# Mixture-of-experts tail of a fused kernel: a second row buffer for the second layer's output, another dealing of the weight splits, and more GpSimd drains

## The chip, the core and the metric

The kernel runs on one core of one Trainium2 chip. The metric is the device time of one execution in microseconds (us), median of several runs. All times below are in us unless ns is written. The engines are called as in the profile: PE is the matrix engine, PEld its weight loads, DVE the vector engine, ACT the scalar engine, POOL the GpSimd engine, SP the engine that issues most DMAs.

## What is computed

Attention with a compressive memory, then two mixture-of-experts layers in a row. Each layer sends every one of 2304 tokens (512 wide) to one of 8 experts and applies that expert's two matrices:

```python
def _moe2_ref(x, w_gate, w1, w2):              # the first layer differs in its router
    logits = x @ w_gate
    expert_idx = np.argmax(logits, axis=1)
    probs = softmax(logits)
    gate_w = probs[np.arange(N), expert_idx]
    for e in range(E):                          # E = 8, D = 512, F = 1024
        mask = expert_idx == e
        h = np.maximum(x[mask] @ w1[e], 0.0)
        out[mask] = gate_w[mask, None] * (h @ w2[e])
    return out

x = attention(...)            # 2304 x 512
x = _moe_ref(x, ...)          # first layer
return _moe2_ref(x, ...)      # second layer
```

## The kernel before, in words

Each layer (`L` = 0 for the first, 1 for the second) is a row of steps `t` = 0, 1, 2, ...; a step takes 128 rows of one expert. The rows of an expert are gathered by index, so the number of steps depends on the data; in the profiled execution there are 22 in each layer, t = 0 to 21. From t = 18 on, a step stands inside a conditional block, since it may not be needed.

A step (`step`, L1508) multiplies its rows by W1 in two halves (PE accumulates in `ph0` and `ph1`), transposes the result (`hT_pe`), and multiplies it by W2 (accumulated in `py`). To keep float32 accuracy every product is made from a high and a low part: `h` and `l` in the code. So each expert's W1 and W2, once they have come by DMA into `stg` in four chunks each, are *split*: ACT writes the high part of a chunk to `Wh` (`split_hi`, L942) and DVE the low part to `Wl` (`split_lo`, L945). There are two sets of `Wh` and `Wl`, so that the next expert's are written while the present one's are read. Splits stand in conditional blocks (`splits`, L1365, the condition at L1370): only the steps before a change of expert do them. A split chunk costs both engines time, and each engine works through its instructions strictly in the order of the program.

W1's four splits are made one step late, in three places of the next step. I number the places: the **first** at the step's start (L1521, ahead of the evacuation of `ph0` into `hs[0]` at L1530), the **second** after the next step's rows were transposed (L1542), the **third** after `hT_ev(1, ...)` (L1563). Before the change chunks 0 and 1 are done in the first place, chunk 2 in the second, chunk 3 in the third. This holds in both layers, for t from 3 to 17 in the first and for t from 3 on in the second (`shifted`). W2's four splits come later in the same step, all at once (L1588 and following). In the first layer the router of the second layer runs between the third place and W2's splits: `route2` (L1424), a chain of small DVE operations (`mn` L1429, `t8s` L1430) with one ACT operation (`th`, L1435), which starts from the step before's output rows.

At a step's end `end(L, t)` (L1458) scales `py` by the gate into the row buffer `ysb` (ACT, L1460) and POOL sends it out. A step with at most 64 rows is a *half step*: two quarter-work halves are computed, ACT copies one (L1468), DVE adds and scales (L1470, L1471). In the second layer POOL scatters `ysb` to the output by an indirect DMA (L1476) and then, at the start of the next step, gathers the rows for the step after that: four transfers into `xg` (L1211) and one into `xca` (L1212), which holds gate and index. All of POOL's DMAs stand in this one order. The next write of `ysb` waits until the scatter from it has landed. Because the two ways of writing `ysb` stand in conditional blocks of ACT and DVE, the scatter waits until both engines have passed them (L1465, L1469), and each gets there only after all that stands ahead of it in its own order.

In the last step that is sure to run (L = 1, t = 16, the 17th) POOL executes a drain ahead of `end` (L1608 to L1610).

`xg0` is a row buffer of the same size as `ysb`; it takes the gathered rows of step 0 of a layer, and nothing uses it after the second layer's step 0 has transposed them.

Of the kernel before, what the change touches and what calls it, by code (L numbers as in the profile page):

```python
# [11 lines left out]
I32 = mybir.dt.int32  # L12
AF = mybir.ActivationFunctionType
ALU = mybir.AluOpType
# [375 lines left out]
def tile_kernel(ctx, tc, q, k, v, M_prev, z_prev, beta, emb, tau, w1a, w2a, wg, w1b, w2b, out):  # L390
    nc = tc.nc
# [3 lines left out]
    P = 128  # L395
    KD, KF = DM // P, FF // P
    NT1 = NTOK // P
# [11 lines left out]
    x1, x2, a1, a2 = x1a[1:], x2a[1:], a1a[1:], a2a[1:]  # L409

    def ctile(shape, name, dt=F32):
        return cst.tile(shape, dt, name=name)
# [9 lines left out]
    xg0 = ctile([P, DM], "xg0")  # L422
# [803 lines left out]
    psx, pm1, ph1, pt0, pt1, py, pm0, ph0 = (psp.tile([P, 512], F32, name=x) for x in ("psx", "pm1", "ph1", "pt0", "pt1", "py", "pm0", "ph0"))  # L1226
# [42 lines left out]
    HT = P // 2  # L1269
# [187 lines left out]

    def end(L, t):  # L1458
        xc = xca[t % 3 if t else 3]
        whole = lambda: nc.scalar.activation(out=ysb, in_=py, func=AF.Copy, scale=xc[:, 0:1])  # L1460
        hv = steps[L, t].hv
        if hv is None:
            whole()
        else:
            with tc.If(hv[1] < 1) as cmp:  # L1465
                whole()
            with cmp.Else():
                nc.scalar.activation(out=ysb[0:HT], in_=py[HT:P], func=AF.Copy)  # L1468
            with tc.If(hv[0] > 0):  # L1469
                nc.vector.tensor_tensor(out=ysb[0:HT], in0=py[0:HT], in1=ysb[0:HT], op=ALU.add)  # L1470
                nc.vector.tensor_scalar(out=ysb[0:HT], in0=ysb[0:HT], scalar1=xc[0:HT, 0:1], scalar2=None, op0=ALU.mult)  # L1471
        if L == 0:
            nc.gpsimd.tensor_copy(xcb, xc)
            nc.gpsimd.dma_start(out=x2[P * t:P * t + P], in_=ysb)
        else:
            nc.gpsimd.indirect_dma_start(out=out, out_offset=bass.IndirectOffsetOnAxis(ap=xc[:, 1:2].bitcast(I32), axis=0), in_=ysb, in_offset=None,  # L1476
                                         bounds_check=NTOK - 1, oob_is_err=False)

    def hT_pe(i, b):
# [28 lines left out]
    def step(L, t):  # L1508
# [9 lines left out]
        before = steps[L, t - 1]  # L1518
        shifted = 2 < t <= (NT1 - 1 if L == 0 else NS - 1)
        if shifted:  # L1520
            before.splits(0, (0, 1), later=True)  # L1521
        if s.hv is None:
            s.gemm(0, ph0, lx, 0, 0, 3)
            yield
# [14 lines left out]
            yT_pe()  # L1539
            yT_ev(b.hs[0])  # L1540
        if shifted:
            before.splits(0, (2,), later=True)  # L1542
        yield
        rk = L == 0 and 2 <= t <= NT1 - 2
        if rk:
# [14 lines left out]
        s.either(lambda: (s.gemm(1, py, lh, 0, 0, n2), hT_pe(1, b)), lambda: (s.gemm2(1, py, lh, 0, HQ[1][0:4]), hT2_pe(1, b)))  # L1560
        hT_ev(1, b, s.hv)
        if shifted:
            before.splits(0, (3,), later=True)  # L1563
            before.loads(0, range(4))
        if more:
            next_flags(L, t + 1)
# [38 lines left out]
        if more:  # L1605
            steps[L, t + 1].pe_flags()
        last_mm[1] = s.lm
        if (L, t) == (1, NT1 - 2):  # L1608

            nc.gpsimd.drain()  # L1610
        if rt2:
            nc.gpsimd.dma_start(out=a2[P * (t - 1):P * t], in_=xcb)
        end(L, t)
        if rk and ((t - 1) % 6 == 0 or t == NT1 - 2):
            c0 = (t - 2) // 6 * 6
# [122 lines left out]
    ysb = fp.tile([P, DM], F32, name="ysb")  # L1738
# [31 lines left out]
    run(C, 1)  # L1770
    g2b(3)
    end(0, 0)
    next_step(0, 1)
    last_mm[0] = last_mm[1] = s.lm
# [7 lines left out]
    for t in range(1, NS):  # L1782
        if t == NT1 - 1:
            nt_ = rg["nt"] = nc.values_load(ini[0:1, 0, 3:4], min_val=NT1, max_val=NS)
        if t >= NT1:
            nest.enter_context(tc.If(nt_ > t, label=f"tile0_{t}"))
        goes_on(0, t)
        if t == 1:
            abreast(step(0, t), C, (6, 0, 11, 2, 0, 0, 4, 20))
        elif t == 2:  # L1790
            abreast(step(0, t), flags_words(fls[0]), (1,))
        elif t == NT1 - 1:
            rg["wv"] = nc.values_load(ini[0:1, 1, 4:5], engines=[ACT_, DVE_], min_val=0, max_val=1)
            steps[1, 0] = Step(1, 0)
            abreast(step(0, t), choose2(), (5, 3, 0, 1, 2, 1, 1, 1, 1, 1, 1, 1, 0))
        else:
            drain(step(0, t))
# [61 lines left out]
    for i, q_ in enumerate(range(3, 24, 3)):  # L1859
        run(C, n1[4 + i])  # L1860
        if i == 3:
            next_rows(1)
        s.gemm(1, py, lh, 0, q_, q_ + 3)
    end(1, 0)
    next_step(1, 1)
    nest = ExitStack()
# [44 lines left out]
```

## Time and profile before

| what | value |
|---|---|
| median of 3 runs | 864.61 us (863.68 to 866.53) |
| the profiled execution, whole | 866.82 us |
| its span, first to last instruction | 865.1 us |
| PE busy share of the span | 96% |
| DVE, ACT, POOL busy share | 64%, 55%, 52% |
| mean granted clock of PE | 0.995 |

In the profile a row of a timeline gives the start in us from the span's start, the busy time, the engine, the line of the kernel, the operation, what it writes and reads, and how many instructions are merged (x4: four); in square brackets stands how long the engine sat idle before it, and what ended that idle time. An engine's name with a q (ACTq, DVEq) means its sequencer: a branch or a wait that it passed. The first layer's steps run from about 298 to 587 us of the span, the second's from about 603 to the end.

### The profile page before, as it was taken

Reading aid. Unit: us, or ns where it says so; the run is one execution under the profiler, and the core shown is the slowest. Engines: PE = TensorE matmul, PEld = TensorE weight load, DVE = VectorE, ACT = ScalarE, POOL = GpSimd, SP = SyncE. Lnnn points to the kernel's source line nnn. Section 1 sums busy time; section 2 is a strip of 40 time slices with the busy share of each in tenths; the row PEclk is TensorE's granted clock in tenths of the full one; section 3 lists DMA queues with packets and bytes.
Section 4 is the critical chain, followed back from the end, with each engine's and each line's share of the span. In section 5 each row is a group of like instructions: output and inputs, shape, how many; then the busy total and the mean of one; then the engine's idle time right before and its main releaser. Section 6 shows DMA issues by size and latency. Waiting matters only on the chain. (4 is left out here: it accounts for less than half of the span.)

```text
span 865.1 us, 21374 instructions
## 1 busy us (share of the span) xinstructions
PE 827.9 (96%) x5091; PEld 634.3 (73%) x5091; DVE 557.9 (64%) x1671; ACT 478.3 (55%) x940; POOL 448.9 (52%) x526
## 2 busy tenths in 40 slices
PE   5999999999999999999999999998999999999995
PEld 2777777777778778777777777776778878677774
DVE  5666667568686987597747776754676625656721
ACT  3666766766757636475636543632385535656632
POOL 5466755644643346464544545355554456544553
PEclk9999999999999999999999999999999999999998
DMA  8423545622406265385715315211667713667111
GB/s 135 85 42 70 105 79 155 131 42 44 104 5 217 86 223 164 118 273 193 246 45 152 127 42 169 102 53 40 243 200 273 231 51 113 207 192 232 46 40 41
DMA packets 145001, 110.58 MB, mean 128 GB/s; under 512 B 112430, under 2 KB 112430, under 8 KB 144824
## 3 DMA queue, kind: packets, MB, share of 16 engines
q1 hardware_dynamic: 130680, 85.03, 35.1%
q0 software_dynamic: 11776, 23.23, 8.6%
q8 instruction: 70, 1.15, 0.6%
q14 instruction: 107, 0.88, 0.4%
q10 hardware_dynamic: 2368, 0.30, 0.2%
HBM read 90.32 MB, written 19.25 MB: 127 GB/s over the span
## 5 line engine op out<-in xcount | busy, mean ns | idle before, releaser
L1356 PE MATMUL py<-Wh,b 128*128 (+1 forms) x640 | 217.0, 403 | 2.4 <-DVE b L1254 2.4
L1356 PE MATMUL ph<-Wh,b 128*128 (+1 forms) x624 | 210.4, 399 | 2.6 <-issue 1.1
L1211 POOL DMA_INDIRECT xg<-x_scratch,pos x168 | 174.5, 1039 | 69.0 <-issue 48.6
L945 DVE TENSOR_TENSOR Wl<-stg,Wh 128x1024 f32 (+1 forms) x120 | 145.5, 1220 | 43.7 <-ACT Wh L942 35.5
L1356 PEld LDWEIGHTS py<-Wh,b 128*128 128x128 f32 x640 | 119.9, 188 | 35.8 <-issue 7.5
L1356 PEld LDWEIGHTS ph<-Wh,b 128*128 128x128 f32 x624 | 115.9, 188 | 32.5 <-issue 5.8
L1356 PE MATMUL py<-Wl,b 128*128 (+2 forms) x344 | 130.1, 397 | 0.0
L1356 PE MATMUL ph<-Wl,b 128*128 (+2 forms) x336 | 129.6, 392 | 0.0
L942 ACT ACTIVATE Wh<-stg 128x1024 f32 (+1 forms) x120 | 125.6, 1057 | 5.7 <-DMA stg<-in_moe_w_dram 2.3
L1254 DVE SCALAR_TENSOR_TENSOR b<-pt,b 128x512 fp32r<-128x512 f32 (+1 forms) x86 | 56.1, 653 | 93.7 <-ACTq L1370 52.2
L267 ACT ACTIVATE att<-psat 128x512 f32<-128x512 f32 (+1 forms) x144 | 66.7, 463 | 75.9 <-PE psat L265 75.4
L288 PE MATMUL psav<-vb,att 128*128 128x128 f32 (+1 forms) x640 | 93.9, 281 | 0.2 <-ACT att L267 0.2
L288 PEld LDWEIGHTS psav<-vb,att 128*128 128x128 f32 x640 | 80.4, 191 | 17.0 <-ACT att L267 5.2
L1249 ACT ACTIVATE b<-pt 128x512 fp32r<-128x512 f32 x86 | 51.4, 598 | 60.1 <-PE pt L1481 46.6
L248 ACT ACTIVATE a<-a,mx 128x128 f32<-128x128 f32 (+3 forms) x128 | 71.0, 555 | 6.0 <-DVE mx L213 5.7
L213 DVE CUSTOM_DVE_ANT_0 a<-pss,wmask 128x128 f32<-128x128 f32 (+3 forms) x128 | 60.9, 481 | 14.9 <-PE pss L235 13.4
L300 POOL TENSOR_TENSOR xb<-tmp,memx 128x512 f32<-128x512 f32 x15 | 19.1, 1271 | 98.8 <-DVE tmp L299 67.6
L1356 PEld LDWEIGHTS py<-Wl,b 128*128 128x128 f32 (+1 forms) x344 | 61.5, 181 | 11.4 <-ACTq L1370 1.3
L1356 PEld LDWEIGHTS ph<-Wl,b 128*128 128x128 f32 (+1 forms) x336 | 60.6, 180 | 12.4
L1460 ACT ACTIVATE ysb<-py,xca 128x512 f32<-128x512 f32 x38 | 25.9, 682 | 71.4 <-PE py L1356 54.9
L1476 POOL DMA_INDIRECT out_dram<-ysb,xca x22 | 23.9, 1088 | 77.1 <-issue 29.0
L1212 POOL DMA_INDIRECT xca<-a_scratch,idx x48 | 47.5, 989 | 19.1 <-issue 12.8
(404 smaller groups left out, 1330.3 us busy)
## 6 DMA issues: line engine op xcount, KB each, us to landing
stg<-in_moe_w_dram SPq DMA_DIRECT2D x120, 512.0 KB, 9.8
x_scratch<-ysb POOLq DMA_DIRECT2D x22, 256.0 KB
qkn<-in_q_dram SPq DMA_DIRECT2D x64, 72.0 KB, 2.5
qkn<-in_k_dram SPq DMA_DIRECT2D x60, 72.0 KB, 2.3
vb<-in_v_dram SPq DMA_DIRECT2D x32, 128.0 KB, 2.5
x_scratch<-xb SPq DMA_DIRECT2D x16, 256.0 KB, 2.6
x_scratch<-stg SPq DMA_DIRECT2D x11, 256.0 KB, 4.5
xg<-x_scratch,pos POOLq DMA_INDIRECT x168
```

The costliest lines, as they stand in the source:

```text
L213: nc.vector.tensor_tensor_reduce(out=out, in0=ps, in1=mask, scale=-0.125, scalar=bound, op0=ALU.add, op1=ALU.min, accum_out=m)
L248: nc.scalar.activation(out=a[:, 0:N], in_=a[:, 0:N], func=AF.Exp, scale=-1.0, bias=mx, accum_out=rs_t[pi][:, c, j:j + 1])
L267: nc.scalar.activation(out=att[:, 0:N], in_=ps[:, 0:N], func=AF.Copy)
L288: nc.tensor.matmul(av_t[pi][:, c, j:], att[:, 128 * kb:128 * kb + 128], vn[:, kb, j:, 0:D], start=(kb == 0), stop=(kb == c))
L942: return nc.scalar.activation(out=chunk(Wh, c, wv), in_=stg[:, c].unsqueeze(1), func=AF.Copy).ins
L945: return nc.vector.tensor_tensor(out=chunk(Wl, c, wv), in0=stg[:, c].unsqueeze(1), in1=chunk(Wh, c, wv).bitcast(F32), op=ALU.subtract).ins
L1211: ind(out=xgt[t % 2][:, P * k:P * k + P], out_offset=None, in_=quarter, in_offset=bass.IndirectOffsetOnAxis(ap=ix[:, k:k + 1], axis=0))
L1212: ind(out=xca[t % 3 if t else 3], out_offset=None, in_=aux[L][0:n], in_offset=bass.IndirectOffsetOnAxis(ap=idx[:, L, t:t + 1], axis=0))
L1249: nc.scalar.activation(out=hl[:, :, 0:P], in_=ps, func=AF.Relu if relu else AF.Copy)
L1254: nc.vector.scalar_tensor_tensor(out=o, in0=x, scalar=0.0, in1=h, op0=ALU.max, op1=ALU.subtract)
L1356: mm = nc.tensor.matmul(o, x, W, start=(first and q_ == qs[0]), stop=(last and q_ == qs[-1]))
L1460: whole = lambda: nc.scalar.activation(out=ysb, in_=py, func=AF.Copy, scale=xc[:, 0:1])
```

## The change

Three edits, all in `step` and `end`:

1. In the second layer odd steps write their output rows to `xg0`, even ones to `ysb`.
2. W1's splits are dealt 1, 1, 2 to the three places, where they were dealt 2, 1, 1: chunk 1 moves from the first place to the second, chunk 2 from the second to the third. Both layers.
3. POOL's drain ahead of `end`, which was in step 16 of the second layer alone, is in every step of that layer from 16 on.

```diff
     def end(L, t):
         xc = xca[t % 3 if t else 3]
-        whole = lambda: nc.scalar.activation(out=ysb, in_=py, func=AF.Copy, scale=xc[:, 0:1])
+        y = xg0 if L == 1 and t % 2 else ysb
+        whole = lambda: nc.scalar.activation(out=y, in_=py, func=AF.Copy, scale=xc[:, 0:1])
...
-                nc.scalar.activation(out=ysb[0:HT], in_=py[HT:P], func=AF.Copy)
+                nc.scalar.activation(out=y[0:HT], in_=py[HT:P], func=AF.Copy)
...
-            nc.gpsimd.indirect_dma_start(out=out, ..., in_=ysb, in_offset=None,
+            nc.gpsimd.indirect_dma_start(out=out, ..., in_=y, in_offset=None,
...
     def step(L, t):
...
         if shifted:
-            before.splits(0, (0, 1), later=True)
+            before.splits(0, (0,), later=True)
...
         if shifted:
-            before.splits(0, (2,), later=True)
+            before.splits(0, (1,), later=True)
...
         if shifted:
-            before.splits(0, (3,), later=True)
+            before.splits(0, (2, 3), later=True)
             before.loads(0, range(4))
...
-        if (L, t) == (1, NT1 - 2):
+        if L == 1 and t >= NT1 - 2:
             nc.gpsimd.drain()
```

## Rows read from the trace of the kernel before

**Rows 1.** The page's first part: busy us, share of the span, instructions
```profile
PE 827.9 (96%) x5091; PEld 634.3 (73%) x5091; DVE 557.9 (64%) x1671; ACT 478.3 (55%) x940; POOL 448.9 (52%) x526
```

**Rows 2.** Waits of PE, first layer (297 to 587): total us, times, longest
```profile
PE pt L1481 <- ACT hs L1530: 2.8, 2, 1.8
```

**Rows 3.** Waits of PE, second layer (605 to 866)
```profile
PE pt L1481 <- ACT hs L1530: 2.8, 3, 1.6
```

**Rows 4.** Timeline of DVE, first layer, step 7, from the third place on
```profile
388.38 0.68 DVE L1254 SCALAR_TENSOR_TENSOR b<-pt,b 128x512 fp32r<-128x512 f32 x1
388.98 1.21 DVE L945 TENSOR_TENSOR Wl<-stg,Wh 128x1024 f32 x1
390.11 0.16 DVE L1429 TENSOR_REDUCE mn<-pm 128x1 f32<-128x8 f32 x1
```

**Rows 5.** Timeline of ACT, first layer, step 7 from its third place into step 8
```profile
387.46 1.05 ACT L942 ACTIVATE Wh<-stg 128x1024 f32 x1
390.57 0.27 ACT L1435 ACTIVATE th<-pm,mn 128x8 f32<-128x8 f32 x1 [2.06 <-DVE t8s L1430]
390.74 4.34 ACT L942 ACTIVATE Wh<-stg 128x1024 f32 x4
394.99 0.67 ACT L1460 ACTIVATE ysb<-py,xca 128x512 f32<-128x512 f32 x1
395.84 0.60 ACT L1530 ACTIVATE hs<-ph 128x512 f32<-128x512 f32 x1 [0.18 <-ACTq L1370]
```

**Rows 6.** Timeline of PE, first layer: starts of steps 4, 7 and 8
```profile
343.84 0.60 PE L1481 MATMUL pt<-ident,hs 128*128 128x128 f32 x4
...
382.62 0.44 PE L1481 MATMUL pt<-ident,hs 128*128 128x128 f32 x2 [1.83 <-ACT hs L1530]
...
392.22 0.39 PE L1356 MATMUL ph<-Wh,b 128*128 x1
...
396.50 0.66 PE L1481 MATMUL pt<-ident,hs 128*128 128x128 f32 x4
```

**Rows 7.** Timeline of ACT, first layer: the same `hs` of steps 4 and 16
```profile
342.93 0.60 ACT L1530 ACTIVATE hs<-ph 128x512 f32<-128x512 f32 x1 [0.18 <-ACTq L1370]
...
502.97 0.60 ACT L1530 ACTIVATE hs<-ph 128x512 f32<-128x512 f32 x1 [0.18 <-ACTq L1370]
```

**Rows 8.** Timeline of ACT, second layer: ends of steps 11 and 17
```profile
737.61 0.67 ACT L1460 ACTIVATE ysb<-py,xca 128x512 f32<-128x512 f32 x1
738.47 0.60 ACT L1530 ACTIVATE hs<-ph 128x512 f32<-128x512 f32 x1 [0.19 <-ACTq L1370]
...
810.30 0.67 ACT L1460 ACTIVATE ysb<-py,xca 128x512 f32<-128x512 f32 x1
811.45 0.60 ACT L1530 ACTIVATE hs<-ph 128x512 f32<-128x512 f32 x1 [0.47 <-PE ph L1356]
```

**Rows 9.** Timeline of ACT, second layer: ends of steps 12 and 16
```profile
747.96 0.60 ACT L1468 ACTIVATE ysb<-py 64x512 f32<-64x512 f32 x1 [3.73 <-DMA out_dram<-ysb,xca]
...
797.09 0.60 ACT L1468 ACTIVATE ysb<-py 64x512 f32<-64x512 f32 x1 [3.65 <-DMA out_dram<-ysb,xca]
```

**Rows 10.** Timeline of PE, second layer: step 13's stall, then step 17's
```profile
751.77 0.44 PE L1481 MATMUL pt<-ident,hs 128*128 128x128 f32 x2 [1.57 <-ACT hs L1530]
...
800.69 0.66 PE L1481 MATMUL pt<-ident,hs 128*128 128x128 f32 x4 [0.72 <-ACT hs L1530]
```

**Rows 11.** Timeline of POOL, second layer: around the drain, and the last two steps
```profile
797.24 0.95 POOL L1212 DMA_INDIRECT xca<-a_scratch,idx  x1 [0.85 <-DMA out_dram<-ysb,xca]
803.84 1.94 POOL L1476 DMA_INDIRECT out_dram<-ysb,xca  x1 [5.66 <-DVE xTs L1244]
...
845.10 1.02 POOL L1476 DMA_INDIRECT out_dram<-ysb,xca  x1 [4.90 <-ACTq L1370]
...
851.49 0.96 POOL L1212 DMA_INDIRECT xca<-a_scratch,idx  x1 [0.30 <-issue]
857.45 1.02 POOL L1476 DMA_INDIRECT out_dram<-ysb,xca  x1 [5.01 <-ACTq L1879]
```

**Rows 12.** Instructions of L1610, the drain: ns min/median/max, first and last start
```profile
L1610 POOLq DRAIN  x1: 4852/4852/4852, 798.0 to 798.0; - x1
```

**Rows 13.** Instructions of L1905, where the kernel ends: POOL's drains
```profile
L1905 POOLq DRAIN  x3: 46/109/2578, 861.7 to 864.8; - x3
```

**Rows 14.** Timeline of DVE beside the drain of step 16
```profile
799.54 2.54 DVE L945 TENSOR_TENSOR Wl<-stg,Wh 128x1024 f32 x2 [0.63 <-ACT Wh L942]
```

More of the change, by code (lines that the diff above doesn't have):

```diff
@@ L1467, in end @@
             with cmp.Else():
-                nc.scalar.activation(out=ysb[0:HT], in_=py[HT:P], func=AF.Copy)
+                nc.scalar.activation(out=y[0:HT], in_=py[HT:P], func=AF.Copy)
             with tc.If(hv[0] > 0):
-                nc.vector.tensor_tensor(out=ysb[0:HT], in0=py[0:HT], in1=ysb[0:HT], op=ALU.add)
-                nc.vector.tensor_scalar(out=ysb[0:HT], in0=ysb[0:HT], scalar1=xc[0:HT, 0:1], scalar2=None, op0=ALU.mult)
+                nc.vector.tensor_tensor(out=y[0:HT], in0=py[0:HT], in1=y[0:HT], op=ALU.add)
+                nc.vector.tensor_scalar(out=y[0:HT], in0=y[0:HT], scalar1=xc[0:HT, 0:1], scalar2=None, op0=ALU.mult)
         if L == 0:
             nc.gpsimd.tensor_copy(xcb, xc)
-            nc.gpsimd.dma_start(out=x2[P * t:P * t + P], in_=ysb)
+            nc.gpsimd.dma_start(out=x2[P * t:P * t + P], in_=y)
         else:
-            nc.gpsimd.indirect_dma_start(out=out, out_offset=bass.IndirectOffsetOnAxis(ap=xc[:, 1:2].bitcast(I32), axis=0), in_=ysb, in_offset=None,
+            nc.gpsimd.indirect_dma_start(out=out, out_offset=bass.IndirectOffsetOnAxis(ap=xc[:, 1:2].bitcast(I32), axis=0), in_=y, in_offset=None,
                                          bounds_check=NTOK - 1, oob_is_err=False)
```

## The prediction

> **What bounds the kernel now.** I read the page's busy shares first: PE is busy for 96% of the span, far ahead of the others [rows 1]. So an edit can only gain what PE still waits for, and can lose whatever it makes PE wait for. Next I read PE's waits by layer. The largest is the same in both: the transposes `pt` of a step wait for ACT's `hs`, 2.8 us in the first layer and 2.8 in the second, in five places [rows 2, 3]. That is the whole purse for edits of ACT's order. Then I followed ACT, DVE and POOL through the steps that split weights, since the change touches only those and the last five. The last thing to see is the end: after the last matmul ACT scales the rows, POOL starts the last scatter at 857.45, and the span ends at 865.1, 7.65 us later [rows 11]; the last scatter's start sets the end one to one.
>
> **Which steps split.** W1's splits fall in steps 3, 6, 7, 9, 13 and 15 of the first layer and in 3, 4, 6, 11, 13, 15 and 17 of the second. The change moves one chunk from the first place of each to the second and another from the second to the third. It adds no split and takes none away; per chunk it shifts 1.05 us of ACT [rows 5] and, by the distance of the next DVE start, 390.11 - 388.98 = 1.13 us of DVE [rows 4] from ahead of the third place to behind it.
>
> **What the first place gives back.** A chunk less ahead of `hs` helps only where PE stalls there. Of the five stalls one is in a step that splits right behind another one (first layer, step 7, 1.83 us [rows 6]), as is step 4 of the second layer. There the chunk that leaves the first place (1.05) is replaced by the one that the step before now does later (1.05 to 1.13): nothing is gained, and 0.1 may be lost. One stall is in step 19 of the first layer, which the dealing does not reach. The other two, 1.57 and 0.72 us in steps 13 and 17 of the second layer [rows 10], follow a half step whose row buffer was late: ACT's write of `ysb` stood 3.7 us until the scatter of the step before had landed [rows 9]. With two buffers that scatter has a whole further step, and with one chunk instead of two ahead of `hs` as well, both stalls go: **-2.29 us**. What is late next in these steps is PE's own `ph0`, which is no wait.
>
> **What the third place costs in the first layer.** Here the extra low split goes straight ahead of the router's chain. DVE has no gap there: `b` ends at 389.06, the one low split fills the time until `mn` starts at 390.11 [rows 4]. ACT seems to have room, for it sits idle 2.06 us ahead of `th` [rows 5]; but it waits there for DVE, and W2's four splits are queued behind `th`. So `th` comes 1.13 later, the W2 splits (4.34 us without a gap), the write of `ysb` and the next step's `hs` come 1.13 later too: these are back to back, with 0.18 us of branches between [rows 5]. PE stands right behind: `pt` of step 8 starts at 396.50, 0.66 after `hs` starts [rows 5, 6]. The `hs` of the steps behind 3, 7, 9, 13 and 15 has this form, with the same 0.18 (first and last of the five [rows 7]). In step 4 `hs` at 342.93 and `pt` at 343.84 are 0.91 apart, so 0.25 of slack is there and 0.88 is lost; in steps 8, 10, 14 and 16 all 1.13; in step 7 the 0.1 of above. Together 0.88 + 4 x 1.13 + 0.1 = **+5.5 us**. Bounds: 0, if DVE's chain were not what `th` waits for, which the gapless rows speak against; and 6 x 1.13 = 6.8 with no slack anywhere.
>
> **What it costs in the second layer.** No router stands between, so ACT runs the splits of the third place and of W2 back to back, and one more makes `ysb` 1.05 later. Where the next step is a full one, ACT then has about 1 us before PE's `ph0` is ready, and nothing is lost (0.1 at most, steps 5, 7 and 14). Where the next is a half step, `ph0` is ready earlier: behind steps 11 and 15 `hs` follows `ysb` with 0.19 us of branches, so 1.05 each; behind step 17 `hs` waited 0.47 for PE, of which some 0.3 is usable, so 0.75 [rows 8]. Sum **+2.85 us**. The bounds are 0 and 3 x 1.05 = 3.15.
>
> **What I cost at nothing.** W1's last low split now ends about 1.1 later; in step 7 that is 391.2, and step 8 first needs W1 at 392.22 [rows 4, 6]. This cover of 1 us hides it; without it PE would stall by what is missing, 0 to 1.1 us per step. SP's loads of the next W1 wait for their chunk's split and start up to 4 us later; in most steps they have a whole step to land, and only steps 3 and 4 of the second layer follow each other so closely that up to 1 us might show. Nothing else moves past them in SP's queue. The scatter also waits for DVE to pass its branch behind the W2 low splits, so it and the gathers behind it in POOL's queue start 1.1 later in split steps; the rows gathered are for two steps on, and the second row buffer takes the late scatter.
>
> **The drains.** POOL gets a drain in steps 17 to 21 between the last gather and the scatter; the scatter and the next five gathers are queued behind it. Only step 16's is in the trace: 4.85 us, of which some 0.15 lies beside the gather from 797.24 to 798.19, and the scatter followed at 803.84 [rows 11, 12]. The nearest other row is POOL's first drain at the kernel's end, 2.58 us, with DVE idle; the two that follow at once take 0.05 and 0.11 [rows 13]. One round on POOL is 6.39 from the scatter to the last gather, 0.96 for this, the drain, and 0.30 of issue [rows 11]. From step 16's scatter, which takes 0.92 longer than the others, to the last one there are 857.45 - 803.84 - 0.92 = 52.7 us for five rounds, 10.54 each; so 2.89 us of drain per round are hidden by the idle time ahead of the scatters (4.9 and 5.0 us [rows 11]). At 2.58 the drains are hidden; at 4.7 each round is 12.35 and the end moves by 5 x 1.81 = 9.1. Step 16's drain ran while DVE did two low splits [rows 14], and only step 17 of the later ones has such work beside it. I take 4.7 for step 17 and 2.58 for the rest: 12.35 + 4 x 10.23 = 53.3 against 52.7, **+0.6 us**. Downwards the bound is 2.5 of gain, if the drains that are now hidden leave the one at the kernel's end as short as the two behind it.
>
> The scatter beside a low split (the one at 803.84) took 1.94 us where the others take 1.02 [rows 11]. The Trainium skill, "SBUF — State Buffer", section "Who interferes with whom", says that a DVE instruction with two SBUF inputs blocks a GpSimd instruction that reads SBUF, since both need one shared read port, while PE and ACT never wait on anyone. By that rule step 16's drain is long because of DVE, and the later ones are short; the longer scatter agrees. The same section infers that the writing of DMA descriptors isn't blocked by such an instruction; by that the drains would stay at 4.85, which is the first rival below.
>
> **Sum.** -2.29 + 5.5 + 2.85 + 0.6 = +6.7 us. Against the profiled execution's own 866.82 that is 873.5; the median of the runs lies 2.2 lower, so 864.61 + 6.7 = **871.3 us**.
>
> **Rivals.** *Each drain keeps its length:* +9.1 instead of +0.6 gives 879.8; drains between the two give 872 to 879. For it speaks that step 16's is the only one in place; against it the shorter one at the end. *The moved chunk is hidden in the first layer:* ACT's 2 us ahead of `th` swallow it, and what remains is -2.29 + 2.85 = +0.6 and the drains: 865.2 to 865.8. Against it stand DVE's rows without a gap. *Faster:* the moved chunk is hidden in both layers and the drain at the kernel's end has less left to do: 864.61 - 2.29 - 2.5 = 859.8. Its place is the drain at the end [rows 13]; it decides if that one falls below some 0.3 us and if DVE had over 1.1 us of slack ahead of `mn`. *The end alone gets shorter,* with the other costs as forecast: 868.2.
>
> **How the numbers follow.** The forecast has 0.48, the long drains 0.22, the hidden chunk 0.15, faster 0.07, the short end 0.08. About 0.3% (2.6 us, so 862.0 to 867.2) is what a measurement of this kernel tells from no change. The first two and the last are slower by more: 0.78; the hidden chunk is within: 0.15; the fourth is faster: 0.07. For 8 in 10 the range goes from 865.0 to 878.0; it leaves out the faster case and the longest drains.
>
> **What would show it.** In the first layer `th` about 1.1 later against PE's step, no gap on DVE ahead of `mn`, and `pt` of steps 8, 10, 14 and 16 with stalls of over 1 us. In the second, no wait of ACT for the scatter, PE's stalls in steps 13 and 17 gone, and half steps 12, 16 and 18 longer by 0.7 to 1.05. POOL's drains near 2.6 from step 18 on, and the last scatter within 1 us of the last `ysb`. I am wrong if `th` stays in place (the first layer's cost falls), or if the last scatter starts long after its rows (the drains cost).

## The result and the profile after

The changed kernel takes 874.51 us (median; 873.15 to 876.86) against 865.56 for the kernel before (four runs, with the three above): ratio 1.0103 [1.008, 1.0126], 8.95 us slower. The prediction was 871.3, between 865.0 and 878.0, slower. The profiled execution takes 873.95 us with a span of 872.2 and a granted clock of 0.997; the kernel before had 866.82, 865.1 and 0.995. So the two traces differ by 7.1 us of span, and these are what the rows below divide up.

First PE's waits after the change, first layer (290 to 590) and then second layer (605 to 873); columns: us in total, times, longest.

```profile
PE pt L1482 <- ACT hs L1531: 9.4, 7, 2.0
```

```profile
PE pt L1487 <- ACT hs L1531: 3.3, 3, 1.4
PE py L1356 <- DVE b L1254: 1.9, 5, 0.5
PE pt L1482 <- ACT hs L1531: 0.8, 2, 0.5
```

In the first layer the wait for `hs` went from 2.8 us in two places to 9.4 in seven [rows 2]. In the second layer the total of 2.8 in three places [rows 3] is now 4.1, and it changed its line: L1487 is the transpose of a half step, and no half step had waited for `hs` before.

Steps are measured on PE from first matmul to next first matmul. Only those that changed by over 0.2 us stand here (before, after):

| step | first layer | step | second layer |
|---|---|---|---|
| 4 | 13.17, 14.08 | 2 | 12.11, 12.41 |
| 8 | 14.70, 16.02 | 5, 7, 14 | 12.05, 12.77; 12.11, 12.47; 13.11, 13.76 |
| 10 | 13.86, 16.73 | 12, 16, 18 | 10.11, 11.40; 10.37, 11.48; 10.19, 11.17 |
| 14 | 15.29, 16.45 | 13 | 13.99, 12.24 |
| 16 | 14.19, 15.55 | 17 | 13.41, 12.44 |
| 19 | 14.54, 14.96 | | |
| all | +7.9 | all | +2.8 |

The step in which the layers change is 1.4 shorter (15.88, 14.44), the attention ahead of the layers 0.4 longer, and from the start of the last scatter to the end of the span it is 2.6 less (7.65, 5.02). Together 7.9 + 2.8 - 1.4 + 0.4 - 2.6 = 7.1.

**The first layer** loses where the prediction looked. DVE's timeline from the third place of step 7 on, after the change:

```profile
389.74 0.68 DVE L1254 SCALAR_TENSOR_TENSOR b<-pt,b 128x512 fp32r<-128x512 f32 x1
390.33 2.53 DVE L945 TENSOR_TENSOR Wl<-stg,Wh 128x1024 f32 x2
392.78 0.16 DVE L1429 TENSOR_REDUCE mn<-pm 128x1 f32<-128x8 f32 x1
```

and ACT's timeline of the same stretch into step 8, which starts on PE at 393.58:

```profile
389.02 2.15 ACT L942 ACTIVATE Wh<-stg 128x1024 f32 x2
393.23 0.27 ACT L1435 ACTIVATE th<-pm,mn 128x8 f32<-128x8 f32 x1 [2.06 <-DVE t8s L1430]
393.41 4.34 ACT L942 ACTIVATE Wh<-stg 128x1024 f32 x4
397.65 0.67 ACT L1461 ACTIVATE ysb<-py,xca 128x512 f32<-128x512 f32 x1
398.50 0.60 ACT L1531 ACTIVATE hs<-ph 128x512 f32<-128x512 f32 x1 [0.18 <-ACTq L1370]
```

and PE's transposes of step 8:

```profile
399.15 0.66 PE L1482 MATMUL pt<-ident,hs 128*128 128x128 f32 x4 [1.34 <-ACT hs L1531]
```

Two low splits now stand without a gap between `b` and `mn`. `th` was 1.65 us ahead of step 8's start [rows 5, 6] and is now 0.35 ahead of it: 1.30 later. ACT's idle time ahead of `th` is 2.06 as before, although ACT does one split more there: it was never room, it was a wait for DVE. The four W2 splits, `ysb` and `hs` follow without a gap, and PE waits 1.34.

**The second layer.** Behind the full splits of step 4 the chain of splits got longer by one, first on ACT, then on DVE (step 5 starts at 660.90; ACT, then DVE):

```profile
656.90 6.51 ACT L942 ACTIVATE Wh<-stg 128x1024 f32 x6
663.32 0.67 ACT L1461 ACTIVATE ysb<-py,xca 128x512 f32<-128x512 f32 x1
664.17 0.60 ACT L1531 ACTIVATE hs<-ph 128x512 f32<-128x512 f32 x1 [0.19 <-ACTq L1370]
```

```profile
657.99 2.54 DVE L945 TENSOR_TENSOR Wl<-stg,Wh 128x1024 f32 x2
660.98 5.17 DVE L945 TENSOR_TENSOR Wl<-stg,Wh 128x1024 f32 x4 [0.45 <-DMA stg<-in_moe_w_dram]
666.80 0.69 DVE L1254 SCALAR_TENSOR_TENSOR b<-pt,b 128x512 fp32r<-128x512 f32 x1 [0.64 <-DVEq L1370]
```

The same place before (step 5 starts at 653.67; ACT, then DVE):

```profile
656.66 0.60 ACT L1530 ACTIVATE hs<-ph 128x512 f32<-128x512 f32 x1 [1.16 <-PE ph L1356]
```

```profile
652.40 5.18 DVE L945 TENSOR_TENSOR Wl<-stg,Wh 128x1024 f32 x4 [0.45 <-DMA stg<-in_moe_w_dram]
658.86 0.69 DVE L1254 SCALAR_TENSOR_TENSOR b<-pt,b 128x512 fp32r<-128x512 f32 x1 [1.27 <-ACTq L1370]
```

After the change `ysb` ends 3.1 us into the step, and `hs` follows by the branches' 0.19 us alone, so PE's `ph0` no longer sets it: the 1.16 us that ACT had waited for PE there are used up. DVE's low splits ended 3.9 us into the step before, and DVE then sat idle 1.27 us until ACT was done; now they end 5.25 into it, 0.64 of branches follow (DVEq L1370), and `b`, on which `py` waits, starts at 5.9 instead of 5.2.

**The end.** POOL's drains: the six of steps 16 to 21 (L1611), and the three where the kernel ends (L1906); columns: ns min/median/max, first and last start. Then the last two POOL transfers.

```profile
L1611 POOLq DRAIN  x6: 3783/4938/5951, 807.8 to 859.5; - x6
```

```profile
L1906 POOLq DRAIN  x3: 46/109/125, 870.8 to 871.9; - x3
```

```profile
861.10 0.95 POOL L1212 DMA_INDIRECT xca<-a_scratch,idx  x1 [0.30 <-issue]
867.20 1.01 POOL L1477 DMA_INDIRECT out_dram<-xg,xca  x1 [5.15 <-ACTq L1880]
```

The first drain at the end fell from 2578 to 125 ns [rows 13]. Those in the steps look as long as the one of before [rows 12], but their records start while gathers are still queued: the last one, from 859.51 to 864.59, starts ahead of two gathers, and ends 2.53 us behind the end of the last one (862.05). Step 17's ends 1.64 behind, step 16's 4.66. The last scatter starts at 867.20, 0.28 us behind the end of the last `ysb`, as before the change, so no drain held it up.

### The profile page after: what moved, and what is told of

Read it like the earlier page. It is cut to its first block, busy times and chain, and to the rows that moved or that the text cites. A ratio compares the mean times of both kernels' runs of the same rounds, so it can differ in the third digit from the quotient of the medians.

```text
span 872.2 us, 21361 instructions
## 1 busy us (share of the span) xinstructions
PE 828.7 (95%) x5091; PEld 633.8 (73%) x5091; DVE 557.8 (64%) x1671; ACT 478.3 (55%) x940; POOL 442.4 (51%) x526
## 5 line engine op out<-in xcount | busy, mean ns | idle before, releaser
L1211 POOL DMA_INDIRECT xg<-x_scratch,pos x168 | 171.4, 1020 | 67.8 <-issue 48.7
L945 DVE TENSOR_TENSOR Wl<-stg,Wh 128x1024 f32 (+1 forms) x120 | 145.6, 1220 | 44.3 <-ACT Wh L942 36.0
L265 PE MATMUL psat<-ident,a 128*128 128x128 f32 x320 | 56.6, 277 | 0.7 <-ACT a L248 0.5
L1482 PE MATMUL pt<-ident,hs 128*128 128x128 f32 x304 | 46.4, 275 | 10.5 <-ACT hs L1531 10.2
```

The costliest lines, as they stand in the source:

```text
L265: nc.tensor.transpose(ps[:, 128 * i:128 * i + 128], x, ident)
L945: return nc.vector.tensor_tensor(out=chunk(Wl, c, wv), in0=stg[:, c].unsqueeze(1), in1=chunk(Wh, c, wv).bitcast(F32), op=ALU.subtract).ins
L1211: ind(out=xgt[t % 2][:, P * k:P * k + P], out_offset=None, in_=quarter, in_offset=bass.IndirectOffsetOnAxis(ap=ix[:, k:k + 1], axis=0))
```

## The experiments

Two of the three series below came from chips on which all kernels ran longer, the one before 962.7 and 953.6 us, with PE's granted clock at 0.96 to 0.97; each ratio is taken on one chip against the kernel before there, and from those two series little more than rows that agree on all chips (the drains, the lengths of the half steps) is used. The series with `e7`, `e8`, `e10` and `e11` ran on a chip like that of the first result (kernel before 866.42).

### One part at a time, on the first of the longer chips

`e1_deal_only`: the kernel before, with the new dealing in both layers.

```diff
-            before.splits(0, (0, 1), later=True)
+            before.splits(0, (0,), later=True)
-            before.splits(0, (2,), later=True)
+            before.splits(0, (1,), later=True)
-            before.splits(0, (3,), later=True)
+            before.splits(0, (2, 3), later=True)
```

> Only the dealing 1, 1, 2 in both layers; one row buffer and the one drain as before. Theory (the dealing is the whole cost; buffers and drains only gain): slower than before by 9 to 12 us, since the changed kernel lost 9.8 us up to the last matmul although two stalls of 2.3 us were gone, and the end keeps its 7.6 us from the last scatter to the end of the span. Also the two stalls of steps 13 and 17 of the second layer stay at 1 us or more. Rival (the dealing costs only what the first layer shows, and part of the second layer's loss came with the drains or the other buffer): slower by 6 to 8 us.

974.8 us against 962.7, ratio 1.013 [1.0064, 1.0195]: 12 slower. The first drain at the end took 2578 ns, as before. The half steps 12, 16 and 18 were 11.5, 11.6 and 11.0 long, as after the change; on the same chip they were 10.1 to 10.3 (12) and 10.4 (16) in all kernels with the old dealing. Of the two stalls that were to stay, step 17's did (1.40 us); in step 13 PE no longer waited for `hs`, although ACT's write of `ysb` still stood 4.0 us for the scatter.

`e2_buffers_drains` has the other two parts, `e3_buffers_only` and `e4_drains_only` one each:

```diff
+        y = xg0 if L == 1 and t % 2 else ysb
...
-        if (L, t) == (1, NT1 - 2):
+        if L == 1 and t >= NT1 - 2:
```

> Two row buffers and drains from step 16 on, W1's splits dealt 2, 1, 1 as before. Theory: faster than before by 4 to 5 us: 2.3 us of stalls in steps 13 and 17 gone, and from the last scatter to the end 5.0 us instead of 7.65. First layer like before within 0.5 us. Rival (the drains need the later row writes of the new dealing to be hidden; without them they push the last scatter): the last scatter starts over 1 us after its rows are written, and the gain is under 2 us.

> Two row buffers alone. Theory: faster by 2.0 to 2.8 us, PE's stalls in steps 13 and 17 gone, ACT's wait for the scatter gone in steps 12 and 16; the end as before, 7.6 us from the last scatter. Rival (the waiting moves on, for instance to the scatter, or to the gather of xca that waits for the same scatter): stalls come back elsewhere in the second layer and it is the same within 1 us.

> Drains from step 16 on, one row buffer, dealing as before. Theory: the drain at the kernel's end is short because the ones ahead have left it little: 2.5 to 2.7 us less from the last scatter to the end, none of the added drains on the path, faster by 2 to 2.7 us. Rival (with one buffer the later scatters of steps 17 to 19 hold up the next rows): ACT waits for the scatter in step 18 or 19 by over 1 us, and the gain is under 1.5 us.

964.26 (0.9975 [0.9926, 1.0025]), 964.01 (1.003 [0.9964, 1.0096]) and 963.23 (0.9993 [0.9952, 1.0034]): none can be told from no change on that chip, where 1 us is a tenth of the spread. Their ends can be read: the first drain took 125 ns in `e2` and `e4`, 2578 in `e3`. PE's stalls in steps 13 and 17, which the second buffer was to take away, stayed: 1.27 and 2.24 us in `e2`, 2.63 and 2.25 in `e3`. So the dealing is what makes the kernel slower, and the drains in the steps are what makes the one at the end short; what the buffers are worth in time stayed open.

### Layer by layer, and the order on DVE, on a chip like the first

`e7_deal_first_layer` has the new dealing in the first layer and nothing else; `e8_deal_second_layer` has two buffers, drains, and the new dealing in the second layer:

```diff
-            before.splits(0, (0, 1), later=True)
+            before.splits(0, (0,) if L == 0 else (0, 1), later=True)
```

and so on for the other two places (in `e8` with `L == 1`).

> The kernel before with the 1, 1, 2 deal in the first layer alone. Theory: the second low split on VectorE, issued ahead of the router of steps 4, 8, 10, 14 and 16, makes each of them 0.9 to 1.4 us longer and step 10 up to 2.9; the layer's steps 1 to 20 together +6 to +8, its end up to 1.5 back if the half-clock stretch of the layer change moves into step 10. The second layer and the end as before (stalls of steps 13 and 17 stay, last drain 2.58). Sum +5 to +8 us against the kernel before, ratio 1.006 to 1.009. Rival: most of the loss needs the second layer's deal: then under +3 us.

875.12 against 866.42, ratio 1.0097 [1.0079, 1.0116]: 8.7 slower with nothing else changed, more than the theory's 5 to 8. The trace is 7.9 longer: the first layer 8.6 (steps 4, 8, 10, 14, 16: +0.95, +2.45, +2.83, +1.17, +1.32, with a stretch of 3.4 us at half clock in each of 8 and 10), the change of layers 1.4 shorter, the second layer the same within 0.2 in sum. The attention, which no edit touches, is 1.0 longer in this trace; it has a stretch at half clock too, at 172.6.

> Two buffers and drains, and the 1, 1, 2 deal in the second layer alone. Theory: first layer as before; the stalls of steps 13 and 17 go (-2.7), the end is 2.6 shorter, half steps 12, 16, 18 are 1.0 to 1.3 longer each (+3.4) and the steps after the full splits 5, 7, 14 together +1.7: sum -0.2, from -1.5 to +1 us, ratio 0.998 to 1.001. Rival: the longer steps of the second layer come from what the first layer left behind, not from its own deal: then as two buffers and drains alone, -4 to -5 us.

867.54, ratio 1.0011 [0.9999, 1.0024]: 1.1 slower, 0.1 beyond the theory's bound. The three parts of the second layer together gain nothing. Steps 5, 7 and 14 are longer by 0.76, 0.36 and 0.60, steps 16 and 18 by 1.11 and 0.97, as after the change, with a first layer that is as before: it is the second layer's own dealing. (Step 12 is 4.2 longer in this trace, as PE was granted half its clock from 744.4 to 751.2.)

`e10_both_low_after_router` is the changed kernel with the third place's low splits, and the loads that must follow them, behind the router:

```diff
-            before.splits(0, (2, 3), later=True)
-            before.loads(0, range(4))
+            before.splits(0, (2, 3), "h" if L == 0 else "hl", later=True)
+            if L == 1:
+                before.loads(0, range(4))
...
         drain(gen)
+        if shifted and L == 0:
+            before.splits(0, (2, 3), "l", later=True)
+            before.loads(0, range(4))
```

> The changed kernel, but in the first layer the third place gives ScalarE the two high splits only, and the two low splits and the loads come behind the router's VectorE work. Theory (the low splits ahead of the router make the first layer longer): steps 4, 8, 10, 14, 16 fall back to within 0.3 us of the kernel before, the layer is 6 to 8 us shorter than in the changed kernel, and the time is 1 below to 2 us above the kernel before. Rival: the high split on ScalarE ahead of the row eviction is what costs: then steps 8, 10, 14, 16 stay 1 us or more longer and the time stays 5 us or more above. Second rival: the late low splits hold up the next step's first matmuls, with waits of TensorE for Wl of over 0.5 us each.

873.91, ratio 1.0086 [1.007, 1.0102]: 7.5 slower than the kernel before, where the theory had at most 2. Of the five steps only step 4 fell back; steps 8, 10, 14 and 16 stayed 0.9 to 1.7 longer, which by the times alone would speak for the first rival. The waits tell the two apart. PE's, in the first layer:

```profile
PE ph L1356 <- DVE Wl L945: 6.4, 5, 1.5
PE pt L1482 <- ACT hs L1531: 1.3, 1, 1.3
```

and DVE's timeline from step 7's router into step 8:

```profile
391.40 7.57 DVE L945 TENSOR_TENSOR Wl<-stg,Wh 128x1024 f32 x6 [0.17 <-issue]
```

With the low splits out of its way the wait for `hs` fell from 9.4 us in seven places to 1.3 in one, so the split ahead of the router did cause it, and the high splits on ACT did not. But six low splits, W1's two and then W2's four, now ran from 391.40 to 398.97, past the start of step 8 (392.60), and PE waited for W1's low part instead: 6.4 us in five places, the second rival. So the theory's cause stood, and its time fell. The two orders lose the same time at different ends. What is short is DVE itself, between the third place and the next step's first matmuls.

`e11_buffers_drains_again` repeats `e2` on this chip:

> Two buffers and drains with the old deal 2, 1, 1, again. Theory: stalls of steps 13 and 17 gone (-2.3 to -2.7), the end 2.6 shorter: -4 to -5.4 us, ratio 0.994 to 0.9955. Rival: without its stalls the second layer's steps 13 and 17 wait for something else, or drains push the last scatter: under -2.5 us.

863.10, ratio 0.9955 [0.9937, 0.9973]: 3.3 faster, between the theory's 4 to 5.4 and the rival's under 2.5, and the only version of this series that beat the kernel before. In its trace, which is 1.9 shorter, the end gives 2.7 (7.65 to 4.97 from last scatter to end of span) and step 2 takes 0.9 back. The buffers gave far less than expected: steps 13 and 17 went from 13.99 and 13.41 to 12.80 and 14.17, -0.4 together. ACT's timeline at step 17 (it starts at 796.06) says why, here in `e11`, then the same place after the change (step 17 starts at 805.53):

```profile
795.83 0.59 ACT L1469 ACTIVATE ysb<-py 64x512 f32<-64x512 f32 x1 [2.16 <-PE py L1356]
798.80 2.15 ACT L942 ACTIVATE Wh<-stg 128x1024 f32 x2 [2.38 <-SPq L1387]
```

```profile
805.30 0.59 ACT L1469 ACTIVATE ysb<-py 64x512 f32<-64x512 f32 x1 [2.16 <-PE py L1356]
807.08 1.06 ACT L942 ACTIVATE Wh<-stg 128x1024 f32 x1 [1.19 <-SPq L1387]
```

The wait for the scatter is gone in both (3.65 before [rows 9]; 2.16 now, on PE, which ends the half step). But the first place's split then waits for SP (L1387, the condition of `loads`). SP's timeline in `e11`:

```profile
784.30 0.33 SPq L1192 DMA_DIRECT2D stg<-in_moe_w_dram  x1
787.37 2.88 SPq L1194 DMA_DIRECT2D stg<-in_moe_w_dram  x4
```

L1192 loads W1, L1194 W2. The split is W1's, and the last of W1's chunks had been issued at 784.30. What SP waits for as it passes over a `loads` that has nothing to load (L1387) are the four W2 loads behind it: they were issued from 787.37 on, and the last of SP's waits with any length ended at 798.60, 11.2 us later. In the kernel before this was 787.14 and 797.12, hidden behind the late `ysb`. So the split stands behind loads that it does not read. Two chunks behind that wait cost more than one: `hs` is 4.9 into step 17 in `e11`, 3.1 after the change.

Against `e8`, which differs by the second layer's dealing alone, `e11` is 4.4 faster. So the parts are +8.7 (first layer's dealing), +4.4 (second layer's) and -3.3 (buffers and drains), 9.8 in sum, where the whole change measured 8.95.

### Drains and two more dealings, on the other longer chip

`e13_drains_only_again` is `e4` once more; `e5_no_drain` is the kernel before with `if False:` in place of the drain's condition.

> The kernel before with the five more drains, one output buffer, old deal. Theory: the drains run while GpSimd has nothing else to do; the last drain falls from 2578 to 125 ns and the semaphore step ahead of it from 0.8 to 0.2, so the end is 2.5 to 2.7 shorter and nothing else moves: -2.3 to -2.8 us, ratio 0.9968 to 0.9975. Rival: a drain that ends late delays a scatter of steps 18 to 21, and with one buffer ScalarE or VectorE waits for it: gain under 1.5 us.

946.66 against 953.58, ratio 0.9893 [0.9841, 0.9946]. That is 7 to 10 us, of which the end explains 2.5; the rest is unexplained, and `e4` did not show it. The first drain at the end took 125 ns again.

> The kernel before without its one drain of step 16; buffers and deal as before. Theory: the length of the last drain follows what was issued since the one before it (125 ns after 3 transfers, 2578 ns after 31, 4.7 us from the end of the last gather after 268): with all of layer 2's transfers behind it, the last one takes 4.5 to 5 us and the time is 1.9 to 2.4 us above the kernel before. Rival: 2578 ns is what any drain at the end takes that has more than a few transfers before it: last drain within 0.2 us of 2.58, time within 0.5 us of before.

958.72, ratio 1.0014 [0.9975, 1.0052]: neither no change nor the 1.9 to 2.4 us of the theory can be ruled out. Its first drain at the end took longer than both theories said:

```profile
L1906 POOLq DRAIN  x3: 55/109/7176, 955.2 to 962.9; - x3
```

From the last scatter to the end it is 13.08 us, where the other three kernels of the series, whose drains stand in steps 16 to 21, have 5.1. The semaphore step ahead of the drain grew as well. By transfers of POOL's since the drain before (in brackets the semaphore step): 3 give 125 ns (0.21 us), 31 give 2578 ns (0.81), 299 give 7176 ns (1.93). So the length of a drain grows with what was issued since the last one, less than in proportion, and it does so with DVE idle. The time since the last drain grows along with the count (6 us, 59 us, the whole kernel), and the runs don't tell which of the two sets it.

`e9_low_after_router` has two buffers, drains, the old dealing, and in the first layer chunk 3's low split alone behind the router; `e12_two_in_the_middle` has two buffers, drains, and 1, 2, 1 in the second layer:

```diff
-            before.splits(0, (0, 1), later=True)
+            before.splits(0, (0, 1) if L == 0 else (0,), later=True)
-            before.splits(0, (2,), later=True)
+            before.splits(0, (2,) if L == 0 else (1, 2), later=True)
```

> Two buffers and drains, old deal 2, 1, 1, but in the first layer the third place gives ScalarE the high split of chunk 3 only; its low split and the loads come behind the router's VectorE work. Theory: the low split that is ahead of the router is what leaves the two waits of hs (3.1 us in the first layer); with one low split behind the router none of the next step's matmuls waits for it over 0.3 us: 1 to 3 us faster than two buffers and drains alone, -4.5 to -6.5 against the kernel before, ratio 0.9925 to 0.995. Rival: as with both low splits behind the router, waits for Wl of about 1.2 us each take the place: no gain over two buffers and drains (-2.5 to -4), or a loss.

> Two buffers and drains, and in the second layer alone the deal 1, 2, 1: the chunk that left the first place goes to the middle one. Theory: the half steps 12, 16, 18 and the steps after full splits (5, 7, 14) fall back to the kernel before within 0.3 us; steps 13 and 17, where the split waits for its load (step 17: 2.4 us with two chunks in the first place), are 12.3 to 13.4 long: -4.5 to -6 us against the kernel before, and 1 to 2.5 faster than two buffers and drains with the old deal. Rival: the second hs follows the middle split directly, so every full step with splits gets up to 1.06 longer: -2 to -3.5.

955.06 (0.9998 [0.9952, 1.0043]) and 953.15 (0.9998 [0.9964, 1.0032]): no gain that can be seen on that chip, and both theories' gains lie outside these intervals. In `e9` no wait of `pt` for `hs` is left among the first layer's larger ones, but `py` waits for DVE's `b` 15.4 us in nine places, against 4.9 in four in `e13` on the same chip: the wait moved once more. In `e12` the half steps were short again (12 and 16: 10.1 and 10.3), and the second `hs` of steps 13 and 17 followed the middle splits without a gap, with waits of 0.5 and 0.6 for it. Whether either would gain on a chip like the first wasn't tried.

## Why the prediction came out as it did

**The third place in the first layer** (forecast +5.5, measured +7.9). The mechanism held row by row: no gap ahead of `mn`, `th` late, `hs` late, and steps 4, 14 and 16 at +0.91, +1.16 and +1.36 where 0.88, 1.13 and 1.13 were forecast; step 8 at +1.32. `e7` shows that the loss is the first layer's, `e10` that it is the low split's. Step 7 lost nothing (0.1 forecast). What was mis-sized is step 10: +2.87 instead of 1.13. Its `pt` starts 1.32 later, as in the other steps; the rest, 1.48, comes a little later in the step, where PE was granted half its clock. From the windows view (length, PE's busy time and instructions, granted clock, DMA share, GB/s), after the change:

```profile
430.40:433.80 3.40, 3.40 (x16) 0.50 1.06 405
```

The kernel before had a stretch of 3.4 us at half clock at 586.8, in the change of layers, which is 1.4 shorter without it. The two just about cancel, so 6.5 of net loss in the first layer and its end stands against 5.5. In `e10`, which has a half-clock stretch neither here nor there, step 10 is 1.73 longer and the change of layers 1.55 shorter. `e8` and `e11`, whose first layer is the old one, have it in the change of layers, `e7`, with the new one, in steps 8 and 10. That the dealing moved it is not shown by this, since `e7` has one more in the attention and `e8` a longer one in step 12 of the second layer. Why PE got it where is open; in the changed kernel a wait of PE of 1.33 ended 2 us ahead of it. A further 0.42 came in step 19, which I have no cause for; in `e7` it is -0.14.

**Two buffers and one chunk less in the first place** (-2.29; -2.72 in steps 13 and 17). The sum was right, its reason half so. The prediction took the scatter as what held these steps up and the chunk as an extra. `e11` shows that the buffers with the old dealing give 0.4: behind the scatter stood SP's wait for the W2 loads. In step 17 of the kernel before it ended within 0.1 us of the scatter, and so was in no row of a wait; in step 13 its trace has 0.39 us of it, ahead of the split at 748.95 (`<-SPq L1387`), a sign that I overlooked. Only with one chunk left behind that wait do both stalls go.

**The third place in the second layer** (half steps +2.85, measured +3.38; others at most 0.1 each, measured +1.73 in steps 5, 7 and 14). The half steps came within 0.25 each of their terms, and above the bound of 3.15. The others are the step that failed: I gave ACT's `hs` 1 us of room there, and did not look at DVE's `b`. Neither held. With one split more, `hs` follows the write of the rows by the branches' 0.2 us alone in all three steps, and `pt` starts 0.12, 0.11 and 0.40 later in steps 5, 7 and 14. And the six low splits ahead of `b`, instead of five, push it past the time at which `py` needs it: `py` starts another 0.59, 0.16 and 0.24 later.

**What was cost at nothing.** The cover of W1's last low split held: in step 7 it ends at 392.86, 0.7 ahead of step 8's start, and no wait of PE for `Wl` is among those of the changed kernel; `e10` shows what it costs once that cover is gone, 6.4 us. Nor does a wait for the later W1 loads stand out in steps 3 and 4 of the second layer, whose lengths are unchanged.

**Drains** (+0.6; measured 0 in the steps and -2.6 at the end). This failed in size and sign. I took 4.7 us for step 17's, since DVE was splitting beside it; its end lies 1.64 behind the last gather. Nor are the records from step 18 on, 3.8 to 6.0 us, near the 2.6 that I had named as a sign. I gave the shorter end 0.15 in the two cases that had it. What I had missed is that step 16's drain had 268 transfers before it: `e5` and the ends of the others show a drain longer the more it has behind it. That DVE's low splits made it long isn't borne out: step 17's drain, with two of them beside it, ended 1.64 us behind the last gather, those of steps 18 and 19, with none, 1.66 and 1.58, and the longest drain of all, 7176 ns, ran with DVE idle. The Trainium skill, "SBUF — State Buffer", section "Who interferes with whom", says that a DVE instruction with two SBUF inputs contends with a GpSimd instruction that reads SBUF. The 1.94 us scatter beside a low split [rows 11] agrees with it, and so does the rest of that trace: of the 137 indirect transfers that POOL issued from 586 us on, the 14 that started with over 0.4 us left of such a DVE instruction (L945, L1256) took 1.34 to 1.96 us, 0.8 to 0.9 more than what was left of it, while none of the 105 that started beside none took over 1.03.

**Sum.** Forecast -2.29 + 5.5 + 2.85 + 0.6 = 6.7; in the trace -2.7 + 7.9 + 3.4 + 1.7 - 2.6 - 1.4 (change of layers) + 0.4 (attention) + 0.4 (step 2 and small ones) = 7.1. The near hit is in part luck, since errors of both signs offset each other: 1.7 not counted behind full splits, and about 3 too dear at the drains.

## What to carry to other kernels

Idle time of an engine ahead of an instruction is room only if what it waits for doesn't get later: here 2 us of idle ACT ahead of `th` were DVE's time, and one more DVE operation cost about its length (0.8 to 1.35 us) on PE in five steps. Before a wait is taken away, look for the event that ends next to it: what ends within 0.1 us of it appears in no list of waits and takes its place, here an engine's pass over a branch that waits for loads of another matrix. A queue that is drained as one goes, while its engine has nothing else to do, leaves less to drain at the end.

## What the runs showed of the hardware

- The first GpSimd drain at the kernel's end takes 125 ns after 3 transfers since the last drain, 2578 after 31 and 7176 after 299, the first two the same to the nanosecond in every kernel that had them; the semaphore step ahead of it takes 0.21, 0.81 and 1.93 us.
- An indirect transfer on POOL that started while DVE had over 0.4 us left of an instruction with two SBUF inputs took 0.8 to 0.9 us more than that rest, up to 1.96 us; one that started beside none took 0.95 to 1.03 (kernel before, second layer).
- One stretch of 3.4 us at PE's half clock (1.2 instead of 2.4 GHz) costs 1.4 to 1.6 us here (change of layers with and without it, and step 10), and it stands in different places in different traces.
- The same kernel took 866 us on one chip and 953 to 963 on two others. Of that nearly nothing lies in the attention (the first step starts at 282 to 287), some 50 us in the first layer and some 35 in the second, with more half-clock stretches and branches of up to 0.7 us where they had at most 0.16. The cause wasn't looked for.
